# Gate, up and their gradients with rows on the partitions, turned by DMA in the first and the last phase of a layer's forward and backward pass

## The chip, the cores and the metric

The kernel runs on one NeuronCore of a Trainium2 chip. The metric is the device time of one execution in microseconds; for each kernel the median of several executions is given.

The engines have the names of the profile. PE is the matrix engine (PEld are its weight loads, the loads of the stationary operand), DVE is the vector engine, ACT the scalar engine, POOL the GpSimd engine, and SP the sync engine, which here only issues DMAs. An engine works through its own queue in order, and what waits at the head of a queue holds up everything behind it.

## The reference

`q`, `k`, `v`, `out` have S = 2048 rows and D = 1024 columns in bf16; the hidden width is F = 3584. The function is one layer, and the kernel gives its output and the gradients of all the inputs that take part:

```python
xn  = layernorm(q)
kv  = shift_conv(k, shift_k) * v              # a causal convolution with 4 taps per column
y   = irfft(rfft(kv) * rfft(ssm_k)) + kv * ssm_D    # a long convolution along the rows
g   = xn @ w_gate ; u = xn @ w_up             # [S, F]
h   = g * u
out = q + (xn * y) * silu(h @ w_down)
# and, for a given grad_out: dq, dk, dv, dshift_k, dssm_k, dssm_D, dw_gate, dw_up, dw_down
```

With `bm = h @ w_down` and its gradient `dbm`, the backward pass of the right-hand branch is `dh = dbm @ w_down.T`, `dg = dh * u`, `du = dh * g`, `dw_gate = xn.T @ dg`, `dw_up = xn.T @ du`, `dw_down = h.T @ dbm`, and `dxn` gets `dg @ w_gate.T + du @ w_up.T`. These matrix products are most of the work of PE. The long convolution is done as a transform in two steps, matmuls with tables and products on DVE.

## The kernel before

A matmul on PE sums over the partitions of its two operands. The stationary operand is at most 128 x 128; the moving one has up to 512 columns here; the result has the columns of the stationary operand on its partitions. So `h @ w_down` needs h with features on the partitions (`hT`), `h.T @ dbm` needs h with rows on the partitions; `xn.T @ dg` needs dg with rows on the partitions, `dg @ w_gate.T` needs it with features on the partitions. Each of h, dg and du is therefore needed in both layouts, and somebody has to turn it.

The 2048 rows are 16 blocks of 128 (`NB`), D is 8 chunks of 128 (`DC`), F is 28 chunks of 128 (`NF`) or 14 slabs of 256 (`NSL`, `SLW`). The time is spent in stages, one after the other on PE:

1. *Start*, 0 to 98.8 us. The layer norm runs over chunks of 2, 2, 4, 4 and 4 row blocks, on DVE and ACT; PE turns each normed block (`XNT`, columns of xn on the partitions, one tile for 4 row blocks), and the first two slabs of gate and up follow chunk by chunk. `load_bcast` spreads the convolution taps and `ssm_D` over the partitions by ten matmuls with a single row (line 149); it comes ahead of the first layer norm. `hrow`, `ssm_k` rows, is turned by PE transposes (line 628).
2. *Gate and up*, 98.8 to 570.4 us, slabs 2 to 13. `gu_unit` (lines 555 to 578) works on one chunk of 128 features and a half of the rows: a weight chunk stands in PE, 512 rows of `XNT` move, the result has features on the partitions. ACT copies it into `gut`, which goes to DRAM (`GUTd`, ACT's queue); DVE multiplies the two halves to `hT`, which goes to DRAM (`HTd`, POOL's queue). After each group of matmuls `tick` issues a share of the forward convolution (`make_pump`): DVE products, transform matmuls, and their DMAs, mostly on POOL's queue.
3. *Down matmul*, 570.4 to 773 us: `bm` from `HTd` (`bm_mm`, line 952) with w_down in the tiles `WD`, which lie in the buffers U6, U7, U2, U3, U9, U10 and U8; `gate` does silu and its derivative and stores `dbm`; PE turns dbm into `DBMT`.
4. *dh and dw*, 773 to 1474.6 us, slab by slab. `dh_half` (lines 1045 to 1071) loads g and u (`gul`), computes dh with features on the partitions (`wdt`, a transposed slab of w_down, is stationary, 512 rows of `DBMT` move), ACT copies it, DVE multiplies (line 1061, inside the helper on line 196). A deferred `turn` stores the products to `DGUTd` on ACT's queue, turns them by 16 PE transposes (line 1069) and two ACT copies (line 1070). `dw_slab` (lines 1073 to 1086) then computes dw_gate and dw_up of the slab from the turned tile. The half slab ahead is always computed before the `dw_slab` that uses the older ones. `btick` issues shares of the backward convolution between the groups; that is mostly work of DVE.
5. *dw_down*, 1474.6 to 1680.8 us: `h` with rows on the partitions comes from `HTd` by DMA transposes (`load_h`, line 1097). Towards its end, w_gate and w_up are loaded by DMA transposes (`WGU`, line 1136).
6. *dx*, 1680.8 us to the end: for each row block, 14 pieces of 4 x 2 matmuls (line 1203), with dg and du loaded from `DGUTd` (`load_dgut`), then `ln_backward` on DVE and ACT. The small matmuls of dk are put between.

`defer` and `flush` push a piece of work back by one or two groups of matmuls. `ld` issues on SP's queue, `st` and `cld` on POOL's, `sta` on ACT's; all DMA transposes go through SP's queue. Within an engine the order is what a scheduler makes of the program's order and of priorities (`high_priority`, `issue_after`). Most big operands live in buffers `U0` to `U10` of 8 KB a partition, each of which has one content after another; a load into one of them waits for the last reader of the content before.

## Time and profile before

| what | us |
|---|---|
| median of four executions | 2105.4 |
| the four executions | 2104.5, 2113.41, 2101.2, 2106.29 |
| the profiled execution | 2105.87 |
| its span | 2104.1 |

The mean clock granted to PE in the profiled execution was 0.993 of the full one. Times in the profile count from the start of the span. "Busy" of a group of instructions is the time in which its engine worked on it; matmuls overlap their neighbours, so a group's mean (379 ns for a matmul of 512 columns) is longer than the distance from one to the next. A line such as `L196` can be that of a helper that many places use; then the operands' names tell them apart. In the lines of groups, the last column is the time for which the engine had nothing to do just before an instruction of the group, with what ended it. Transfers are listed with their queue and with the median time from issue to landing.

### The profile page before, as it was taken

Reading aid. Unit: us, or ns where it says so; the run is one execution under the profiler, and the core shown is the slowest. Engines: PE = TensorE matmul, PEld = TensorE weight load, DVE = VectorE, ACT = ScalarE, POOL = GpSimd, SP = SyncE. Lnnn points to the kernel's source line nnn. Section 1 sums busy time; section 2 is a strip of 40 time slices with the busy share of each in tenths; the row PEclk is TensorE's granted clock in tenths of the full one; section 3 lists DMA queues with packets and bytes.
Section 4 is the critical chain, followed back from the end, with each engine's and each line's share of the span. In section 5 each row is a group of like instructions: output and inputs, shape, how many; then the busy total and the mean of one; then the engine's idle time right before and its main releaser. Section 6 shows DMA issues by size and latency. Waiting matters only on the chain.

```text
span 2104.1 us, 28251 instructions
## 1 busy us (share of the span) xinstructions
PE 2031.7 (97%) x11242; PEld 1033.7 (49%) x11242; DVE 1451.3 (69%) x1950; ACT 677.3 (32%) x1028; POOL 300.9 (14%) x448
## 2 busy tenths in 40 slices
PE   5999999999999999999999999999999999999998
PEld 4445555556444445555444444544444444444443
DVE  7779898978555556777999877987786025344432
ACT  4633433334333343444333343333122202111111
POOL 2211111110011120001021112111111101110100
PEclk9999999999999999999999999999999999999999
DMA  7666676456497877667788777756955995444431
GB/s 245 208 235 198 212 231 215 165 200 234 168 337 248 259 252 238 191 210 175 252 251 238 212 223 233 238 188 195 256 148 155 244 288 174 154 153 161 152 105 41
DMA packets 412789, 435.51 MB, mean 207 GB/s; under 512 B 178176, under 2 KB 326952, under 8 KB 401648
## 3 DMA queue, kind: packets, MB, share of 16 engines
q1 hardware_dynamic: 260816, 184.84, 31.0%
q0 software_dynamic: 40768, 174.40, 24.1%
q10 hardware_dynamic: 111072, 74.47, 11.7%
q8 instruction: 88, 1.44, 0.3%
q14 instruction: 45, 0.37, 0.0%
HBM read 221.78 MB, written 179.34 MB: 191 GB/s over the span
## 4 chain that ended last, share of the span: by engine, by line
PE 47%; DVE 24%; issue 19%; DMA 6%; POOL 2%; ACT 1%; SPq 1%; ACTq 0%; POOLq 0%; DVEq 0%
PE psx L1203 18%; PE psb L1170 9%; DVE m L196 7%; PE psg L565 7%; DVE W L196 5%; PE psb L1077 5%; DVE HX L196 3%; DMA B<-HFd 2%; PE psP L213 2%; PE psS L213 1%; PE psdk L927 1%; PE psb L1054 1%; DVE A L196 1%; DVE KX L196 1%; DVE B L196 1%
## 5 line engine op out<-in xcount | busy, mean ns | idle before, releaser
L565 PE MATMUL psg<-U,wslab 128*128 128x512 bf16 (+1 forms) x1856 | 406.7, 375 | 7.7 <-ACT guts L567 4.1
L1077 PE MATMUL psb<-U,U 128*128 128x512 bf16 x1792 | 399.6, 379 | 0.0
L1203 PE MATMUL psx<-U,dgut 128*128 128x512 bf16 x1408 | 308.5, 379 | 0.0
L565 PEld LDWEIGHTS <-wslab 128*128 128x128 bf16 x1856 | 182.8, 99 | 198.8 <-issue 9.2
L1203 PEld LDWEIGHTS <-dgut 128*128 128x128 bf16 x1792 | 175.3, 98 | 211.4
L1077 PEld LDWEIGHTS <-U 128*128 128x128 bf16 x1792 | 173.9, 98 | 194.2
L1054 PE MATMUL psb<-U,wdt 128*128 128x512 bf16 x896 | 208.1, 383 | 1.1 <-ACT bm L967 1.1
L1170 PE MATMUL psb<-U,U 128*128 128x512 bf16 x896 | 197.2, 379 | 2.8 <-DMA U<-HTd 2.8
L567 ACT CAST gut<-psg 128x512 bf16<-128x512 f32 x192 | 112.5, 587 | 223.5 <-PE psg L565 217.1
L952 PE MATMUL psbm<-U,ht 128*128 128x512 bf16 x784 | 171.8, 379 | 0.0
L1081 ACT CAST wb<-psb 128x512 bf16<-128x512 f32 x112 | 65.7, 587 | 267.3 <-PE psb L1077 225.0
L196 DVE TENSOR_TENSOR m<-A,B 128x1024 bf16<-128x1024 bf16 (+1 forms) x160 | 116.7, 793 | 44.1 <-issue 18.6
L196 DVE TENSOR_TENSOR W<-W 128x1024 f32<-128x1024 f32 (+1 forms) x144 | 139.5, 986 | 2.9
L1170 PEld LDWEIGHTS <-U 128*128 128x128 bf16 x896 | 86.7, 98 | 104.3 <-DMA U<-HTd 3.8
L1054 PEld LDWEIGHTS <-wdt 128*128 128x128 bf16 x896 | 87.5, 99 | 96.2 <-issue 5.5
L1226 ACT ACTIVATE dx_t<-dxn 128x1024 bf16<-128x1024 f32 (+1 forms) x17 | 17.1, 1007 | 345.4 <-DVE dxn L196 338.5
L952 PEld LDWEIGHTS <-ht 128*128 128x128 bf16 x784 | 76.1, 98 | 89.0
L196 DVE TENSOR_TENSOR dka<-dkh,Wbc 128x1024 bf16<-128x1024 bf16 x16 | 11.1, 692 | 156.9 <-DMA dkh<-DKSHd 156.9
L1070 ACT COPY U<-tr 128x1024 bf16<-128x1024 bf16 x112 | 109.4, 1022 | 17.7 <-PE tr L1069 6.1
L1056 ACT CAST dht<-psb 128x512 bf16<-128x512 f32 x112 | 65.3, 587 | 119.3 <-PE psb L1054 77.7
L196 DVE TENSOR_TENSOR gul<-gul,dht 128x2048 bf16<-128x2048 bf16 x56 | 69.6, 1243 | 29.9 <-ACT dht L1056 29.4
L1203 PE MATMUL psx<-W,dgut 128*128 128x512 bf16 x384 | 86.0, 379 | 0.0
(240 smaller groups left out, 2432.3 us busy)
## 6 DMA issues: line engine op xcount, KB each, us to landing
gul<-GUTd SPq DMA_DIRECT2D x56, 512.0 KB, 6.0
DGUTd<-gul ACTq DMA_DIRECT2D x56, 512.0 KB, 7.4
dgut<-DGUTd SPq DMA_DIRECT2D x16, 1792.0 KB, 8.6
GUTd<-gut ACTq DMA_DIRECT2D x48, 512.0 KB, 4.5
A<-DYFd POOLq DMA_DIRECT2D x16, 1024.0 KB, 5.7
out_dram<-wb ACTq DMA_DIRECT2D x224, 64.0 KB, 3.1
ht<-HTd SPq DMA_DIRECT2D x7, 1536.0 KB, 7.4
KFd<-KX POOLq DMA_DIRECT2D x8, 1024.0 KB, 4.5
```

The source lines that it names most:

```text
L196: V.tensor_tensor(o, a, b, op)
L213: nc.tensor.matmul(ps[:, k].rearrange("p (c d) -> p c d", c=2), T[:, r, k, :], xr[:, r], start=(n == 0), stop=(n == len(rs) - 1))
L565: nc.tensor.matmul(ps[:, 0:n], w[:, dc, a, fi * P:(fi + 1) * P], XNT[q][:, dc, qo:qo + n], start=(dc == 0), stop=(dc == DC - 1))
L567: nc.scalar.copy(out=gut[:, a, o:o + n], in_=ps[:, 0:n])
L952: nc.tensor.matmul(ps[:, dh * 512:(dh + 1) * 512], ht(fc)[:, i * P:(i + 1) * P], WD[fc // 4][:, fc % 4, dh * 512:(dh + 1) * 512], start=(f ...
L1054: nc.tensor.matmul(ps[:], wdt[:, dc, fi * P:(fi + 1) * P], DBMT[2 * hf + k][:, dc, :], start=(dc == 0), stop=(dc == DC - 1))
L1056: nc.scalar.copy(out=dht[:, k * 512:(k + 1) * 512], in_=ps[:])
L1070: nc.scalar.copy(out=dgu[:, :, a, fi * P:(fi + 1) * P], in_=ps[:])
L1077: nc.tensor.matmul(ps[:], XN[b // 4][:, b % 4, dc * P:(dc + 1) * P], dgus[b // 8][:, b % 8].rearrange("p a f -> p (a f)"), start=(b == 0), ...
L1081: nc.scalar.copy(out=wb[:].rearrange("p a f -> p (a f)"), in_=ps[:])
L1170: nc.tensor.matmul(ps[:], h(b, f), DBM[b // 4][:, b % 4, dh * 512:(dh + 1) * 512], start=(b == 0), stop=(b == NB - 1))
L1203: nc.tensor.matmul(ps[:, dh * 512:(dh + 1) * 512], t[a][:, 4 * j + f, i * P:(i + 1) * P], WGU[n][:, f, dh * 512:(dh + 1) * 512], start=(n ...
```

## The change

The rows take the place of the features on the partitions, wherever g, u, h and their gradients are computed.

- `gu_unit` keeps a block of 128 rows of `XNT` in PE and moves 512 columns, the up and the gate part of a slab. g and u go to `GUd`, and h, with rows on the partitions, to `Hd`. `turn_h` reads half a slab of `Hd` (1024 rows x 256 features, 0.5 MB) back by a DMA transpose on SP's queue and stores it to `HTd` on POOL's queue; `h_done` puts this off by one half slab.
- `dh_half` keeps a block of `DBMT` in PE and moves 256 columns of `wdt`: 1792 matmuls of 256 columns instead of 896 of 512. DVE multiplies in place in the tile that held g and u (`DGU`), and `dw_slab` reads that tile. The PE transposes and their copies are gone. The products are stored to `DGd`.
- `load_h` reads `Hd` without turning.
- `load_dgut` turns the gradients: 56 DMA transposes of 0.5 MB in the last phase, 14 for each group of 512 rows. dx works on pairs of row blocks.
- In the start, the products of `load_bcast` come behind the gate/up matmuls of the third and fourth chunk, and the turning of `hrow` behind the last layer-norm transposes.
- Buffers move: `v`, `acc` and `prod` of the convolution lie in U4 and U7, there are two more buffers (U11, U12), PSUM is shared out anew, and the pieces of `WGU` are loaded earlier in dw_down.

The core of the diff:

```diff
-    def gu_unit(fc, s0, ns, w, tick):
...
-                for dc in range(DC):
-                    nc.tensor.matmul(ps[:, 0:n], w[:, dc, a, fi * P:(fi + 1) * P], XNT[q][:, dc, qo:qo + n],
-                                     start=(dc == 0), stop=(dc == DC - 1))
-                nc.scalar.copy(out=gut[:, a, o:o + n], in_=ps[:, 0:n])
...
-        sta(GUTd[fc, :, :, s0:s0 + ns], gut[:, :, 0:ns])
...
+    def gu_unit(sl, b0, n, w, tick):
+
+        gut = fg.tile([P, 4, 2, SLW], BF16, name="gut")
+        hN = fg.tile([P, 4, SLW], BF16, name="hN")
+        for i in range(n):
+            q, qi = divmod(b0 + i, 4)
+            ps = ps_gu.tile([P, 512], F32, name="psg")
+            for dc in range(DC):
+                gu_mm[0] = nc.tensor.matmul(ps[:], XNT[q][:, dc, qi * P:(qi + 1) * P],
+                                            w[:, dc].rearrange("p a f -> p (a f)"), start=(dc == 0), stop=(dc == DC - 1))
+            nc.scalar.copy(out=gut[:, i].rearrange("p a f -> p (a f)"), in_=ps[:])
+            flush(2)
+            tick()
+        sta(GUd[sl, b0 // 8][:, b0 % 8:b0 % 8 + n], gut[:, 0:n])
+        tt(hN[:, 0:n], gut[:, 0:n, 0], gut[:, 0:n, 1], MUL)
+        st(Hd[sl, b0 * P:(b0 + n) * P, :].rearrange("(b u) f -> u b f", u=P), hN[:, 0:n])
+
+    hT_due = []
+
+    def turn_h(sl, hf):
+
+        hT = fg.tile([P, 2, 1024], BF16, name="hT")
+        nc.sync.dma_start_transpose(out=hT[:], in_=Hd[sl, hf * 1024:(hf + 1) * 1024, :])
+        fr = sl % 12 * SLW
+        st(HTd[hf][sl // 12][fr:fr + SLW, :].rearrange("(a f) s -> f a s", f=P), hT[:])
+
+    def h_done(sl, hf):
+
+        hT_due.append((sl, hf))
+        if len(hT_due) > 1:
+            turn_h(*hT_due.pop(0))
...
-    load_bcast(bsb, ps_st)
+    bcast = load_bcast(bsb, ps_st)
...
+        for sl in range(2):
+            gu_unit(sl, b0, n, slabs[sl], nop)
+            if i in (2, 3):
+                with tc.issue_after(gu_mm[0].ins):
+                    for j in ((3, 4), (2,), (1,), (0,))[2 * (i - 2) + sl]:
+                        bcast(j)
...
+    turn_h(*hT_due.pop())
     flush()
     drain()
...
-    def dh_half(fc, hf, wdt, dgu):
...
-            for a in range(2):
-                ps = ps_tr.tile([P, 8, P], BF16, name="tr")
-                for i in range(8):
-                    nc.tensor.transpose(ps[:, i, :], dgt[:, a, i * P:(i + 1) * P], ident[:])
-                nc.scalar.copy(out=dgu[:, :, a, fi * P:(fi + 1) * P], in_=ps[:])
-        defer(turn)
+    def dh_half(k, wdt):
+
+        sl, hf = divmod(k, 2)
+        dgu = DGU[k]
+        for g in range(2):
+            bs = slice(4 * g, 4 * g + 4)
+            dht = bg.tile([P, 4, SLW], BF16, name="dht")
+            for e in range(2):
+                ps = ps_b.tile([P, 512], F32, name="psb")
+                for x in range(2):
+                    b = 4 * g + 2 * e + x
+                    for dc in range(DC):
+                        nc.tensor.matmul(ps[:, x * SLW:(x + 1) * SLW], DBMT[2 * hf + g][:, dc, (b % 4) * P:(b % 4 + 1) * P],
+                                         wdt[:, dc, :], start=(dc == 0), stop=(dc == DC - 1))
+                nc.scalar.copy(out=dht[:, 2 * e:2 * e + 2].rearrange("p b f -> p (b f)"), in_=ps[:])
+                flush(2)
+                btick(1)
+            with tc.high_priority(60):
+                tt(dgu[:, bs], dgu[:, bs], dht[:].unsqueeze(2).to_broadcast([P, 4, 2, SLW]), MUL)
+
+        def store():
+            fs = slice(sl % 2 * SLW, sl % 2 * SLW + SLW)
             for a in range(2):
...
+                sta(DGd[sl // 2, a, 1024 * hf:1024 * hf + 1024, fs].rearrange("(b u) f -> u b f", u=P), dgu[:, :, a, :])
+        defer(store)
+        return dgu
...
+    def load_h(sl, home):
+        h = u8(home, "p (b f) -> p b f", b=NB)
+        ld(h, Hd[sl].rearrange("(b u) f -> u b f", u=P))
+        return h
...
+    def load_dgut(g, n):
+
+        a, j = pieces[n]
+        t = (gd, gd2)[n // 7].tile([P, 4, 512], BF16, name=f"dgut{n}")
+        nc.sync.dma_start_transpose(out=t[:], in_=DGd[j, a, 512 * g:512 * g + 512, :])
+        return t
...
+    ts = [load_dgut(0, n) for n in range(7)]
+    for i, j in enumerate((11, 0, 1, 4, 5)):
         load_wgu(9 + i, u8(j, a=4))
-    ts[1] = load_dgut(1)
...
+        ts.append(load_dgut(0, 7 + i))
+    ts += [load_dgut(0, n) for n in (12, 13)]
+    for g in range(4):
+        for b in (4 * g, 4 * g + 2):
+            if b == NB - 2:
+                break
+
+            pss = [ps_x.tile([P, D], F32, name="psx") for i in range(2)]
+            for n in range(14):
+                for i in range(2):
+                    dx_part(ts, b % 4 + i, pss[i], n)
+                if b % 4 == 2:
+                    ts[n] = load_dgut(g + 1, n)
+            for i in range(2):
+                with tc.high_priority(40):
+                    ln_backward(b + i, lambda h: pss[i][:])
```

## The prediction

> **What bounds the kernel now.** First the busy totals of the page:
>
> ```profile
> span 2104.1 us, 28251 instructions
> PE 2031.7 (97%) x11242; PEld 1033.7 (49%) x11242; DVE 1451.3 (69%) x1950; ACT 677.3 (32%) x1028; POOL 300.9 (14%) x448
> ```
>
> TensorE (PE) is busy for 97% of the span, so only less matmul work, or the 72 us in which it is idle, can make the kernel faster. Next the same by stage. A row holds the window, its length, then busy time and count of PE, PEld (weight loads), DVE, ACT and POOL, the granted clock, the DMA share and GB/s. The rows are the start, the gate/up phase, the dh/dw phase and the dx phase:
>
> ```profile
> 0.00:25.40 25.40, 8.60 (x45) 4.55 (x46) 19.82 (x68) 10.04 (x18) 8.71 (x20) 0.98 0.98 334
> 98.80:570.40 471.60, 457.76 (x2683) 258.99 (x2681) 406.25 (x518) 180.30 (x303) 71.36 (x114) 0.99 0.61 205
> 773.00:1474.60 701.60, 681.10 (x4073) 351.08 (x4073) 579.84 (x730) 276.32 (x415) 98.72 (x142) 0.99 0.73 223
> 1680.80:2104.10 423.30, 413.87 (x1918) 187.42 (x1916) 164.12 (x214) 57.61 (x86) 38.44 (x61) 0.99 0.48 154
> ```
>
> The average DVE share hides something. Cut into feature slabs, the dh/dw phase has DVE as full as PE in some of them:
>
> ```profile
> 806.20:857.50 51.30, 50.97 (x325) 27.24 (x323) 40.57 (x62) 21.19 (x34) 3.72 (x7) 1.00 0.68 209
> 1006.90:1057.90 51.00, 48.59 (x290) 24.48 (x289) 50.72 (x60) 19.09 (x29) 4.44 (x7) 1.00 0.79 241
> 1107.30:1159.00 51.70, 48.37 (x276) 24.83 (x274) 51.07 (x62) 18.89 (x30) 7.99 (x12) 0.97 0.80 237
> 1006.90:1356.70 349.80, 335.44 (x1937) 170.69 (x1936) 316.44 (x366) 133.76 (x202) 60.37 (x91) 0.99 0.76 230
> ```
>
> Slab 1 (first row) is PE's alone; in slabs 4 and 6 (next two) DVE is busy 50.72 of 51.00 and 51.07 of 51.70 us; the last row is slabs 4 to 10 together. Last, the groups that the change touches (busy time, mean ns; idle time before, and what ended it), and single stretches of PE's and SP's timelines:
>
> ```profile
> L1070 ACT COPY U<-tr 128x1024 bf16<-128x1024 bf16 x112 | 109.4, 1022 | 17.7 <-PE tr L1069 6.1 <-DVE W L196 5.2 <-PE psb L1077 2.8
> L196 DVE TENSOR_TENSOR gul<-gul,dht 128x2048 bf16<-128x2048 bf16 x56 | 69.6, 1243 | 29.9 <-ACT dht L1056 29.4
> L1069 PE MATMUL tr<-ident,gul 128*128 128x128 bf16 x896 | 60.9, 222 | 14.9 <-DVE gul L196 14.9
> L628 PE MATMUL tr<-ident,hrow 128*128 128x128 bf16 x128 | 10.9, 227 | 3.9 <-DMA hrow<-in_A_ssm_k_dram 3.8
> L149 PE MATMUL tr<-wrow,ones_row 1*128 1x512 bf16 x8 | 4.0, 614 | 13.0 <-DMA wrow<-in_A_shift_k_dram 9.0 <-ACT Wbc L150 4.0
> ```
>
> ```profile
> 33.81 7.15 PE L565 MATMUL psg<-U,wslab 128*128 128x256 bf16 x64
> 571.06 24.33 PE L952 MATMUL psbm<-U,U 128*128 128x512 bf16 x112 [0.67 <-ACT gut L567]
> 1064.76 1.06 PE L1069 MATMUL tr<-ident,gul 128*128 128x128 bf16 x16
> ```
>
> ```profile
> 580.56 10.08 SPq L62 DMA_DIRECT2D ht<-HTd  x2
> 1656.08 4.25 SPq L1136 DMA_TRANSPOSE W<-in_B_w_up_dram  x1
> 1660.55 4.20 SPq L1136 DMA_TRANSPOSE W<-in_B_w_gate_dram  x1
> ```
>
> Prices. A 512-column matmul: the chain of waits shows 96 of dx in 20.72 us, 215.8 ns each. A 256-column one with its own weight load: 7.15/64 = 112 ns, 4 ns over half of that. A PE transpose: the next stretch starts 0.89 us after 16 of them, 55.6 ns. A DMA transpose of 1 MB: about 4.2 us on SP's queue, so 2.1 for 0.5 MB.
>
> **The change part by part.** The profiled execution took 2105.9 us (span 2104.1), 0.5 above the median of the four runs; the sum goes against 2105.9.
>
> *Start (0 to 98.8).* The broadcast products (L149) cost PE 13.0 us of waiting ahead of the first gate/up work; they go behind chunks 2 and 3, and the hrow transposes (L628, 3.9 of waiting) behind the last layer-norm transposes. Both waits go, but the layer norm is late next: DVE is busy 19.8 of the first 25.4 us, and its chunks release PE one after the other. I take −7, a little under half of 16.9; ends −13 (the larger wait whole) and 0.
>
> *Gate/up (98.8 to 570.4).* Swapping the stationary operand leaves the count of 512-column matmuls, their copies and products as they are. New are 28 transposes of h on SP (28 × 2.1 = 59 us), 14.7 MB written to Hd, and POOL's wait for each transpose ahead of its store to HTd, with conv loads queued behind. PE's matmuls hide all of it: the DMA share is 0.61, and 59 more of 471.6 make 0.74. A slab's weights are asked for about two slabs ahead, so a transpose ahead of them on SP has a slab (about 34 us) of slack. With the cover gone, each of 28 could cost POOL about 4 us, but only conv loads feel it: ends 0 and +12; I take +3, near the covered end.
>
> *Turn to the down matmul (570.4).* Before, PE goes on after 0.67 us, with half of h long loaded and the last weight tiles (U8 to U10, via SP) just in time. Now the last half slab needs: ACT's copy 0.6, the product 0.7, the store's issue 0.55 and landing about 4.5 (256 KB stores of h: 4.3), the transpose 4 to 5.6, the store to HTd about 5: some 17 us. The last weight loads and the first ht tiles wait on SP behind that transpose, or for its buffer. The weights then land near 570.4 + 21.6; PE, with 13.8 us of matmuls on the earlier tiles, stalls about 7, and a little more for ht: +9. Ends: +6 (half the fill hidden again), and +16, since the last weight issue to ht's landing takes under 24 us in the before trace.
>
> *dh and dw (773 to 1474.6).* Gone are 896 PE transposes, 896 × 55.6 ns = 49.8 us of PE, and 112 ACT copies (109.4 us, off the path); 896 matmuls of 512 columns become 1792 of 256: 896 × 2 × 4 ns = +7 by 7.15/64, a stretch that also holds the fill of the first matmul; two halves at 215.8 give 0. I take +2. PE's 14.9 us of waits for the product lie mostly in slabs 4 to 10, where PE idles for 14.4 us; the weight-gradient matmuls now read the product itself, with a whole dh_half (7 us) between product and use, so elsewhere I add no wait.
> The DMA stores (1 MB per half slab) stay in size; gu loads become 28 of 1 MB instead of 56 of 0.5, issued two and a half slabs ahead.
> What DVE does is unchanged, and decides what of it is won. Slabs 4 to 10: 349.8 us, PE 335.4 − 7/14 × 49.8 + 1 = 312, DVE 316.4. Before, the span exceeded the larger of the two by 14.4 us; add 14 again to DVE's 316: 330, a gain of 20. Ends: 0 (DVE's order, not its total, sets the pace), 34 (no excess). Slabs 0 to 3, where PE alone is full: 4/14 × 47.8 = 14. Slabs 11 to 13: 10 by the same. Sum −44; ends −24 and −58.
>
> [...] The trace has 64 256-column matmuls with their own loads in 7.15 us. [...]
>
> *dw_down (1474.6 to 1680.8).* h comes by plain 1 MB loads instead of transposes, 512 bytes a run. PE is busy 203.35 of 206.2 already. 0; ends −2 and +5 (the first tiles late).
>
> *dx (1680.8 to the end).* The gradients now come by 56 DMA transposes of 0.5 MB: 56 × 2.1 = 118 us of SP in 413 us of PE. At the start 5 weight pieces and 7 gradient pieces need 5 × 4.3 + 7 × 2.1 = 36 us, where PE's first pair of rows offers 45: +1, ends 0 and +10. Later each piece has about 45 us until it is used. Rows go in pairs with 3 PSUM tiles; a pair's turn leaves 3.5 us (16 matmuls) for DVE's first read of 1.2 us: 0. If the pieces were late, PE waits, since nothing else is left but dk.
>
> [...]
>
> Sum: −7 + 3 + 9 − 44 + 0 + 1 = −38; 2105.9 − 38 = 2068.
>
> **The rivals.**
> A, the sum: 2068, own range 2052 to 2084.
>
> B, DVE holds slabs 4 to 10 at the old pace, so 20 of the 44 are lost: DVE's order of conv work and products is what slab 4's 50.72 of 51.00 speaks for; slabs 9 and 10, with DVE at 40 of 50, speak against. With the turn's upper end (+7): 2068 + 20 + 7 = 2095, range 2088 to 2100.
>
> C, all of PE's gain is won, and the start's: 2068 − 14 − 6 = 2048. For: DVE's 29.9 us of waiting before the product (for ACT), which has less to do now. Against: the excess of 14 was there before.
>
> D, slower: the dx phase is bound by its DMA transposes. Its first group of 14 pieces is consumed while the next arrives, and PE spends 4 × 14 × 8 × 0.2158 = 97 us on a group. Up to 97/14 = 6.9 us a piece PE is not held; the same 0.5 MB transposes of w_down took 8.1 us (median) from issue to landing. Should each wait for the one before to land, 56 × 8.1 = 454 us against 388 of dx matmuls: +66, 2134. It eats the whole gain of 38 from (388 + 38)/56 = 7.6 us. Against: consecutive transposes of 1 MB stand 4.2 us apart.
>
> E, no change: as B, and the start gains nothing either, because the layer norm alone sets it (+7): 2102.
>
> **How the numbers follow.** A 50%, B 18%, C 13%, D 11%, E 8%. About 0.5% (10.5 us) is what a measurement of this kernel can tell from no change. A, B and C are faster but for the upper edge of B: 0.79; E and that edge are the same: 0.09; D: 0.12. The range goes from C's lower middle, 2042, to E's upper edge, 2104; it leaves out D and the bottom of C, about 15%. The predicted time is A's.
>
> **What would show it.** PE's busy time near 1984 with no L1069 transposes; ACT near 568; slabs 0 to 3 about 3.5 us shorter each, slabs 4 to 10 about 3 with DVE at 95%; one PE wait of 6 to 16 us at the first down matmuls, ended by a weight load or ht; first gate/up matmuls before 20 us. The prediction is wrong if 256-column matmuls take over 120 ns, if slabs 4 to 10 keep 50 us, or if PE waits in dx for the transposed gradients.

## The result, and the profile after

The changed kernel takes 2116.05 us (median of 40 runs, 2103.03 to 2128.02), the kernel before 2102.86 us (median of 59). The ratio is 1.0058, with a 95% interval of 1.0046 to 1.0069: it is slower by half a per cent, where a gain of 38 us was forecast, and lies outside the range. The profiled execution took 2111.27 us with a span of 2109.1, 5.0 us over the one before.

The page's totals of the changed kernel:

```profile
span 2109.1 us, 28068 instructions
PE 1995.0 (95%) x11178; PEld 1065.8 (51%) x11178; DVE 1459.1 (69%) x1937; ACT 574.5 (27%) x911; POOL 329.5 (16%) x466
```

PE has 36.7 us less to do, and stands idle for 114.1 us instead of 72.4. The same by stage (columns as in the prediction: window, length, PE, PEld, DVE, ACT, POOL, clock, DMA share, GB/s). The windows are gate/up with the forward convolution, the down matmul, dh/dw, and dx:

```profile
88.00:592.00 504.00, 463.78 (x2682) 261.50 (x2683) 411.05 (x522) 180.69 (x304) 101.28 (x141) 0.96 0.82 243
592.00:815.40 223.40, 204.08 (x1027) 95.45 (x1026) 111.71 (x177) 65.29 (x65) 41.52 (x65) 0.97 0.86 272
815.40:1472.40 657.00, 634.63 (x4065) 389.18 (x4064) 581.14 (x721) 170.08 (x300) 97.13 (x139) 0.99 0.76 232
1675.90:2109.10 433.20, 416.36 (x1918) 187.37 (x1916) 164.18 (x214) 57.72 (x86) 38.41 (x61) 0.99 0.64 149
```

| stage | before | after | difference | forecast (ends) |
|---|---|---|---|---|
| start | 98.8 | 88.0 | −10.8 | −7 (−13 to 0) |
| gate/up with conv forward | 471.6 | 504.0 | +32.4 | +3 (0 to +12) |
| turn and down matmul | 202.6 | 223.4 | +20.8 | +9 (+6 to +16) |
| dh/dw | 701.6 | 657.0 | −44.6 | −44 (−58 to −24) |
| dw_down | 206.2 | 203.5 | −2.7 | 0 (−2 to +5) |
| dx | 423.3 | 433.2 | +9.9 | +1 (0 to +10) |

So the gain came where it was expected and in its full size. Most of it was given back in the stages into which the turning was moved, above all in gate/up. There the waits of three engines answer one another. In the changed kernel's list of waits (total, times, longest), PE, DVE and POOL in the gate/up window:

```profile
PE psP L216 <- DVE W L199: 23.4, 4, 9.7
PE psS L216 <- DVE kv L199: 7.9, 1, 7.9
...
DVE U L199 <- DMA k<-KSLd: 29.7, 3, 12.2
...
DVE kv L199 <- DMA U<-in_A_v_dram: 11.4, 1, 11.4
...
POOL HTd L65 <- DMA hT<-Hd: 211.2, 23, 15.4
```

PE stands in the convolution's transforms (line 216 of the changed kernel, 213 of the one before) because DVE is late, DVE is late because loads of k and v are, and POOL, on whose queue these loads are, waits 211 us for transposes of h. In the kernel before, the lists of PE and DVE for the same stage have these two lines, and POOL's has no wait for a turned tile:

```profile
PE psP L213 <- DVE W L196: 5.3, 3, 3.1
...
DVE prod L196 <- DMA k<-KSLd: 11.6, 4, 6.3
```

One such place in the changed kernel's POOL timeline, and what DVE then waited for:

```profile
239.80 0.71 POOL L65 DMA_DIRECT2D HTd<-hT  x1 [12.74 <-DMA hT<-Hd]
240.50 0.58 POOL L65 DMA_DIRECT2D k<-KSLd  x1
```

```profile
254.15 1.23 DVE L199 TENSOR_TENSOR U<-k,Wbc 128x2048 bf16<-128x2048 bf16 x1 [12.22 <-DMA k<-KSLd]
```

A load of k stands right behind the store that waits, and a second one at 244.2 us, in a row of issues that POOL lets go at once. DVE's wait ends when the second lands, 10.0 us after its issue. A PE wait of 9.7 us follows, which ends at 256.6.

The turn to the down matmul, on PE's and on SP's timeline, with the second wait that comes at the other end of this stage:

```profile
605.52 3.61 PE L974 MATMUL psbm<-U,U 128*128 128x512 bf16 x16 [1.92 <-DMA U<-in_B_w_down_dram]
618.27 12.61 PE L974 MATMUL psbm<-U,U 128*128 128x512 bf16 x48 [9.13 <-DMA U<-in_B_w_down_dram]
...
814.57 1.03 PE L1013 MATMUL psb<-ident,dbm 128*128 128x128 bf16 x8 [6.70 <-DVE dbm L199]
```

```profile
600.82 5.23 SPq L581 DMA_TRANSPOSE hT<-Hd  x1
...
612.55 1.49 SPq L62 DMA_DIRECT2D U<-in_B_w_down_dram  x3
```

The last transpose goes off at 600.8, and the last three loads of w_down at 612.6. In dx, PE waits 0.8, 5.1 and 1.6 us for the transposed gradients of its first pair of rows, and nowhere later:

```profile
1717.80 5.50 PE L1222 MATMUL psx<-U,dgut 128*128 128x512 bf16 x16 [5.13 <-DMA dgut<-DGd]
```

### The profile page after: what moved, and what is told of

The parts are those of the page before. It is cut to its first block, busy times and chain, and to the rows that moved or that the text cites. A ratio compares the mean times of both kernels' runs of the same rounds, so it can differ in the third digit from the quotient of the medians.

```text
span 2109.1 us, 28068 instructions
## 1 busy us (share of the span) xinstructions
PE 1995.0 (95%) x11178; PEld 1065.8 (51%) x11178; DVE 1459.1 (69%) x1937; ACT 574.5 (27%) x911; POOL 329.5 (16%) x466
## 4 chain that ended last, share of the span: by engine, by line
PE 41%; DVE 10%; issue 4%; DMA 2%; SPq 2%; POOL 1%; ACT 0%; ACTq 0%; DVEq 0%; POOLq 0%
PE psx L1222 17%; PE psb L1111 10%; PE psb L1191 9%; DVE W L199 4%; PE psb L1092 3%; DVE m L199 2%; SPq L1162 2%; DVE U L199 1%; PE psdk L949 1%; DMA dyl<-DYd 1%; DMA B<-HFd 1%; DVE B L242 1%; DVE A L199 1%; DVE B L199 1%; PE psY L914 1%
## 5 line engine op out<-in xcount | busy, mean ns | idle before, releaser
L567 PE MATMUL psg<-wslab,U 128*128 128x512 bf16 x1792 | 407.8, 382 | 3.3 <-ACT gut L569 1.6
L1222 PE MATMUL psx<-U,dgut 128*128 128x512 bf16 x1536 | 337.8, 381 | 7.5 <-DMA dgut<-DGd 7.5
L1111 PEld LDWEIGHTS <-U 128*128 128x128 bf16 x1792 | 176.1, 98 | 211.4 <-issue 16.7
L567 PEld LDWEIGHTS <-U 128*128 128x128 bf16 x1792 | 175.4, 98 | 199.3 <-issue 10.1
L1092 PE MATMUL psb<-wdt,U 128*128 128x256 bf16 x1792 | 206.0, 275 | 0.0
L569 ACT CAST gut<-psg 128x512 bf16<-128x512 f32 x224 | 130.7, 585 | 247.4 <-PE psg L567 243.3
L1092 PEld LDWEIGHTS <-U 128*128 128x128 bf16 x1792 | 176.2, 98 | 23.6
L1191 PEld LDWEIGHTS <-U 128*128 128x128 bf16 x896 | 86.9, 98 | 102.2
L199 DVE TENSOR_TENSOR dka<-dkh,Wbc 128x1024 bf16<-128x1024 bf16 x16 | 11.1, 692 | 174.5 <-DMA dkh<-DKSHd 174.5
L216 PEld LDWEIGHTS <-TF 128*128 128x128 bf16 x640 | 62.7, 102 | 60.7 <-DVE W L199 29.6
L199 DVE TENSOR_TENSOR U<-U,dht 128x2048 bf16<-128x2048 bf16 x56 | 68.2, 1221 | 23.5 <-ACT dht L1094 23.5
L199 DVE TENSOR_TENSOR gg<-bm,sig 128x1024 bf16<-128x1024 bf16 x16 | 11.0, 690 | 99.9 <-ACT sig L992 99.9
```

The lines of the kernel that those rows point to most:

```text
L199: V.tensor_tensor(o, a, b, op)
L216: nc.tensor.matmul(ps[:, k].rearrange("p (c d) -> p c d", c=2), T[:, r, k, :], xr[:, r], start=(n == 0), stop=(n == len(rs) - 1))
L567: gu_mm[0] = nc.tensor.matmul(ps[:], XNT[q][:, dc, qi * P:(qi + 1) * P], w[:, dc].rearrange("p a f -> p (a f)"), start=(dc == 0), stop=(dc ...
L569: nc.scalar.copy(out=gut[:, i].rearrange("p a f -> p (a f)"), in_=ps[:])
L1092: nc.tensor.matmul(ps[:, x * SLW:(x + 1) * SLW], DBMT[2 * hf + g][:, dc, (b % 4) * P:(b % 4 + 1) * P], wdt[:, dc, :], start=(dc == 0), sto ...
L1111: nc.tensor.matmul(ps[:], XN[b // 4][:, b % 4, dc * P:(dc + 1) * P], dgus[b // 8][:, b % 8].rearrange("p a f -> p (a f)"), start=(b == 0), ...
```

## The experiments

The theories at first: P, that POOL's queue is the cause in gate/up (convolution loads stand behind stores that wait for transposes); T, that the added traffic slows the loads in whatever order; M, that the swapped operands are slower on PE. Later C was added: transposes that are under way together with a burst of other transfers make both crawl. "Gate/up" below runs from the first matmul of slab 2 to the first down matmul, 472.3 us before and 505.1 after (good to some 2 us). Ratios are to the kernel before on the same chip.

**e1, the store of the turned h one half slab later on POOL's queue.**

`store_h` stores the half slab turned before, behind the newest store of h to Hd.

```diff
+            with tc.issue_after(hd_st[0].ins):
+                st(HTd[hf][sl // 12][fr:fr + SLW, :].rearrange("(a f) s -> f a s", f=P), hT)
...
     def turn_h(sl, hf):
 
+        store_h()
         hT = fg.tile([P, 2, 1024], BF16, name="hT")
         nc.sync.dma_start_transpose(out=hT[:], in_=Hd[sl, hf * 1024:(hf + 1) * 1024, :])
-        fr = sl % 12 * SLW
-        st(HTd[hf][sl // 12][fr:fr + SLW, :].rearrange("(a f) s -> f a s", f=P), hT[:])
+        hT_st.append((sl, hf, hT[:]))
```

> The store of the turned h to HTd is queued on POOL one half slab later, behind the next half slab's store of h, when its transpose should long have landed. All transfers and bytes stay. In the changed kernel POOL waits 211 us of the gate/up phase for transposes (88 to 592 us), and gate/up takes 504 us where it took 471.6 before. Theory P (POOL's queue: the convolution's loads of k and v and the stores of h stand behind the waiting store): POOL's wait for transposes falls below 50 us, DVE's waits for k and v (41 us) fall to about the 12 us of before, gate/up takes 470 to 482 us, and the whole is 22 to 34 us faster than the changed kernel, about 2085. Theory T (traffic: 28 transposes and 14.7 MB more keep the loads late, in whatever order): gate/up stays above 495 us, the whole within 10 us of the changed kernel. Theory M (the swapped operands are slower on PE): no change either, and PE busy per matmul stays up where nothing waits.

2102.76 us, ratio 0.9979 (0.9956 to 1.0003): 13 us less than the changed kernel. POOL's wait for transposes fell from 211 to 4.7 us, and from 140 us on no PE wait in gate/up exceeds 4.4 us. But gate/up is still 497.1, above the 495 that was set for T, because one wait of 22.5 us now stands at 110 to 132 us, where a load of k made DVE wait for 21.4. P is right for the later waits; the first one needs another cause.

**e2, no turning of h.** The transposes are left out; HTd gets g and u, straight from ACT's tile.

```diff
-        hT = fg.tile([P, 2, 1024], BF16, name="hT")
-        nc.sync.dma_start_transpose(out=hT[:], in_=Hd[sl, hf * 1024:(hf + 1) * 1024, :])
...
-        st(HTd[hf][sl // 12][fr:fr + SLW, :].rearrange("(a f) s -> f a s", f=P), hT[:])
+        flat = last_gut[0][:].rearrange("p b a s -> p (b a s)")
+        st(HTd[hf][sl // 12][fr:fr + SLW, :].rearrange("(a f) s -> f a s", f=P),
+           flat.rearrange("p (a s) -> p a s", a=2))
```

> Leaves out the 28 transposes of h: HTd gets the same 0.5 MB stores from POOL, but out of the tile of g and u that ACT has just written, so the values in HTd are not h. It shows what the transposes' own traffic costs. Theory P: gate/up takes 468 to 480 us, within 6 us of the late store. Theory T: gate/up falls by 20 us or more against the late store. Theory M: still about 504. At the turn to the down matmul PE's 11.7 us of waiting shrinks to some 3 to 6, since the last store to HTd no longer waits for a transpose.

2065.34 us (two executions), ratio 0.9806 (0.9776 to 0.9837), gate/up 468.9. M falls: the same matmuls with the same operands take no longer than before (472.3). Everything that was lost in gate/up hangs on the turning. The run does not tell P from T, since both the transposes' traffic and POOL's waits for them are gone. That the whole is within 3 us of the forecast is in part chance, as the forecast had 9 us for the turn to the down matmul, of which little is left here either (PE's waits for w_down are 2.7 us instead of 11.1).

**e3, the last half slab turned behind the loads of w_down; the last dbm block turned behind the first dh matmuls.**

```diff
-    turn_h(*hT_due.pop())
...
-    WD += [u8(j, a=4) for j in (2, 3, 9, 10, 8)]
+    WD += [u8(j, a=4) for j in (2, 3, 8, 9, 10)]
...
         ht1 = load_ht(1)
+    sl, hf = hT_due.pop()
+    hT = U[1][:, 0:2048].rearrange("p (a s) -> p a s", a=2)
+    with tc.issue_after(ht1[1].ins):
+        nc.sync.dma_start_transpose(out=hT, in_=Hd[sl, hf * 1024:(hf + 1) * 1024, :])
+    st(HTd[hf][sl // 12]..., hT)
...
-    flush()
     for k in (1, 2):
         gu_in(k)
```

> Only the stage change at 592 us and the one at 808 us are touched. The last half slab of h is turned into a free part of U1 behind the loads of w_down and of the first ht on SP, and the weight tiles are taken in the order U8, U9, U10; the turn of the last dbm block is no longer put ahead of the first dh matmuls. If the wait came from SP's order and from the buffer of the last transpose: PE's 11.7 us of waits for w_down fall to 0 to 3, and the 6.7 us for dbm to under 1.5; from the last gate/up matmul to the first dh matmul 204 to 209 us instead of 223.4; the whole 14 to 20 us faster than the changed kernel, about 2098. Rival (the wait is the late store of h and of y itself, behind POOL's waits, whatever stands on SP): 6 to 10 us of the first wait stay, and the whole gains 6 to 10.

2114.18 us, ratio 1.0033 (1.0011 to 1.0055). Place by place it did what it should: 11.7 us became 2.8, and 6.7 became 1.9 (the dbm turn) and 1.1. From the first down matmul to the first dh matmul it is 211.9 us instead of 222.3. A part came back at once, in e3's PE timeline, as the third row block waits for its dbm, whose inputs now stand behind ht and the last transpose on SP:

```profile
645.01 1.03 PE L1012 MATMUL tr<-ident,dbm 128*128 128x128 bf16 x8 [5.38 <-DVE dbm L199]
```

Some 5 us more came back in dh/dw (662.3 instead of 657.2), which now holds the turn of the last dbm block. So the price of the turn was read rightly, and of the 10 us saved there 2 show in the medians and some 4 in the profiled executions (2106.79 against 2111.27), which the spread does not tell from none.

**e4, dx starts with three row blocks.**

```diff
-        for b in (4 * g, 4 * g + 2):
+        for b, m in ((0, 3), (3, 1)) if g == 0 else ((4 * g, 2), (4 * g + 2, 2)):
...
-                if b % 4 == 2:
+                if b % 4 + m == 4:
                     ts[n] = load_dgut(g + 1, n)
```

> The dx phase only: the first pass takes three row blocks instead of two (5.2 us of PE per piece instead of 3.5), then one alone. If PE's 7.5 us of waits come from the start, where five weight pieces and seven gradient pieces follow one another on SP at some 6 us a pair: no wait is left, dx takes 423 to 427 us instead of 433.2, the whole is 6 to 10 us faster than the changed kernel. If the transposes are bound by their rate throughout: a wait of the same size comes back in the second pass, and the whole stays within 3 us.

2116.76 us, ratio 1.0044 (1.002 to 1.0068): nothing gained. The 7.5 us of waits for gradients are gone, and a wait of 9.9 us, at 1810 to 1820 us, for the dk units' load of dkh has taken their place; dx takes 435.1. The whole stayed where the second expectation had it, but not for its reason.

**e5, late store, and the turning of slabs 0 to 3 put off to slab 4 and later, two in each half slab.**

```diff
-        if len(hT_due) > 1:
+        if sl >= 4 and len(hT_due) > 1:
             turn_h(*hT_due.pop(0))
...
+            if sl >= 4 and len(hT_due) > 1:
+                turn_h(*hT_due.pop(0))
```

> The late store, and besides the first eight half slabs of h are not turned in slabs 0 to 3 but two by two from slab 4 on; transfers and bytes stay. With the late store alone PE still stood for 22.5 us at 110 to 132 us, while loads of k took up to 29 us to land, 256-byte transpose packets took 620 ns instead of 18, and the DMA moved 43 to 190 GB/s. Theory C (collision: three transposes in flight at once with the loads and stores at the start of the convolution make the DMA collapse): the 22.5 us and the slow clock behind it go, gate/up falls from 497 to 468 to 480 us, the whole is 25 to 35 us faster than the changed kernel, about 2085. Theory T (traffic): the transposes cost what they cost, wherever they lie: stalls of that size appear from slab 4 on, and gate/up stays at 488 or more.

The added turn stands between the two `gu_unit` calls of a half slab.

2108.17 us, ratio 1.0034 (1.0004 to 1.0063); gate/up 498.1. From 86 to 197 us, where no transpose of h runs, PE never waits longer than 0.9 us. Then, where two half slabs are turned in the time of one, the store follows its transpose too soon, POOL waits again (up to 15.9 us), and PE stands for 12.5 and 9.1 us. The total looks like T; the places speak for P and for C.

**e6, plain loads in place of the transposes of h** (the values in HTd are not turned).

```diff
-        nc.sync.dma_start_transpose(out=hT[:], in_=Hd[sl, hf * 1024:(hf + 1) * 1024, :])
+        ld(hT[:].rearrange("p a s -> p (a s)").rearrange("p (b f) -> p b f", b=8),
+           Hd[sl, hf * 1024:(hf + 1) * 1024, :].rearrange("(b u) f -> u b f", u=P))
```

> The changed kernel with each DMA transpose of h replaced by a plain load of the same 0.5 MB from the same place into the same tile, in runs of 512 bytes; the stores to HTd and all waits for them stay, so the values in HTd are not turned. Theory P (the wait in POOL's queue as such): POOL waits for the plain loads too, some 100 to 200 us, and gate/up stays at 490 or more. Theory T/C (the transposes, not the bytes): POOL's waits for it shrink to under 60 us, no collapse at 100 to 130 us, gate/up at 468 to 480.

2101.96 us, ratio 0.9995 (0.9971 to 1.002); gate/up 496.2. The list of POOL's waits in e6:

```profile
POOL HTd L65 <- DMA hT<-Hd: 205.8, 24, 14.4
```

POOL waits as long for plain loads as for transposes (211.2). Most of it is spent before the transfer starts, for it in turn waits for the store of h to Hd, which stands on POOL's own queue (SP waits 286.6 us for that in e6). SP's line in the changed kernel's list of waits:

```profile
SPq L581 <- DMA Hd<-hN: 260.5, 27, 27.7
```

Nor do the transfers themselves differ much by the median. From issue to landing the changed kernel's transposes of h have the first line below, and e6's plain loads the second (the last number is the median):

```profile
DMA to landing us min/median/max: 4.1/5.3/13.6
```

```profile
hT<-Hd SPq DMA_DIRECT2D x28, 512.0 KB, 5.1
```

PE stands for waits of 7.1 and 9.4 us that end at 247 and 372 us, as in the changed kernel, and the load of k behind the first of them takes 10.6 us to land with no transpose near it. This is P. At the start of the convolution the two waits are 3.3 and 6.1 us (7.9 and 4.6 with transposes). The kernel is 14 us faster than the changed one, so that turning by transposes does have a price beside that of the queue.

**e7, half of the product in dh** (half of the weight gradients are not gradients).

```diff
-                tt(dgu[:, bs], dgu[:, bs], dht[:].unsqueeze(2).to_broadcast([P, 4, 2, SLW]), MUL)
+                tt(dgu[:, bs, 0], dgu[:, bs, 0], dht[:], MUL)
```

> Leaves out half of the product in dh: only one of the two halves (u) of each tile is multiplied, so half of the weight gradients are not gradients. It takes about 28 us from DVE (56 x 0.5 us) in the dh/dw phase and nothing from PE. If DVE holds slabs 4 to 10 (330.0 us now, PE about 313 busy): those slabs lose 8 to 14 us, the first four slabs and the last three at most 1 to 3 together. If PE and its waits for the weight gradients' operands hold them: slabs 4 to 10 stay within 4 us of 330.

Slabs 4 to 10 in the changed kernel, and then in e7:

```profile
1030.90:1360.90 330.00, 312.64 (x1922) 189.07 (x1920) 316.62 (x368) 81.05 (x144) 60.17 (x93) 0.98 0.81 244
```

```profile
1053.60:1371.50 317.90, 309.50 (x1921) 188.77 (x1921) 296.81 (x360) 80.55 (x146) 59.56 (x91) 0.98 0.82 243
```

Taking 20 us from DVE shortens them by 12.1 while PE has the same matmuls: DVE does hold them. The kernel as a whole was slower, 2140.76 us (two executions; 1.0191, 1.017 to 1.0213), in part for a reason that belongs to the edit. The half that is no longer multiplied can be stored early, and ACT got stuck in issuing such a store, just ahead of the slabs measured above. It is seen on e7's ACT and PE timelines:

```profile
1041.62 11.21 ACTq L68 DMA_DIRECT2D DGd<-U  x1
```

```profile
1053.57 6.80 PE L1111 MATMUL psb<-U,U 128*128 128x512 bf16 x22 [10.61 <-ACT dht L1094]
```

**e8, e5 with e3, and h of dw_down in three buffers instead of four so that one weight piece of dx is loaded at slab 9.**

```diff
-    HSL = (3, 11, 6, 2)
+    HSL = (3, 11, 6)
...
+        if k == 9:
+            load_wgu(6, u8(2, a=4))
```

> The late and spread turning of h, the last half slab turned behind the loads of w_down into U1, the last dbm block turned behind the first dh matmuls, and h of dw_down in three buffers instead of four, so that one more weight piece of dx is loaded at slab 9. By theory C: gate/up 468 to 480, the down stage 206 to 212, dx 427 to 432 us; the whole about 2070 to 2080, faster than both kernels. By theory T: about 2100.

2105.26 us, ratio 0.9994 (0.9964 to 1.0025), gate/up 510.5 with PE waits of 13.4, 8.9 and 10.5 us from 244 us on: no better, as e5.

**e9, the store of the turned h on SP's queue.** One word of the changed kernel.

```diff
-        st(HTd[hf][sl // 12][fr:fr + SLW, :].rearrange("(a f) s -> f a s", f=P), hT[:])
+        ld(HTd[hf][sl // 12][fr:fr + SLW, :].rearrange("(a f) s -> f a s", f=P), hT[:])
```

> The changed kernel with one edit: the store of the turned h to HTd goes out on SP's queue, directly behind its transpose, instead of POOL's. So POOL waits for no transpose, SP does, where only the weights of a slab ahead stand behind; and a transpose is sent off only when the one before has been turned and its store is issued, so that never two or three are under way at once. Transfers and bytes stay. Theory P with C (POOL's queue, and the collision of several transposes with the backlog that it lets go at once): no PE wait over 5 us in the gate/up phase, which takes 470 to 482 us instead of 505, the whole 20 to 33 us faster than the changed kernel, 2083 to 2096. Theory T (the traffic itself, as e6 with plain loads at 496 us could also be read): gate/up stays at 490 or more. If SP takes POOL's place as the one that holds things up: PE waits for wslab.

2086.02 us, ratio 0.9922 (0.9899 to 0.9946): 30 us less than the changed kernel, and faster than the kernel before. (The profiled execution, 2094.88, is among its slowest; the stages are read from it.) The transfers and bytes are the same, and from 131 us on no PE wait in gate/up exceeds 1.9 us, which speaks against T. One wait is left, of 22.9 us at 107 to 130 us, so gate/up takes 490.9 us: not the 482 or less that was expected, and still within the 490 or more set for T. T falls only with e14 and e15, which move the same bytes in 477.8 and 469.1 us. In e9's list of waits, and among its DMA issues at 93 to 110 us (queue, count, size, median us to landing):

```profile
PE psP L216 <- DVE W L199: 24.4, 3, 22.9
```

```profile
k<-KSLd POOLq DMA_DIRECT2D x2, 352.0 KB, 22.5
...
hT<-Hd SPq DMA_TRANSPOSE x1, 30.6
```

The transpose before had landed by then (its store goes off at 94.4 us, this one at 94.9), so here one transpose beside the burst was enough. It is issued at the same time as the loads of k, which POOL no longer holds back: at 95.9 us, where in the changed kernel they left at 112.1.

**e10, e9 with e3 and the earlier weight piece.**

> The store on SP, the last half slab of h turned behind the loads of w_down into U1, the last dbm block turned behind the first dh matmuls, h of dw_down in three buffers so that one more weight piece of dx is loaded at slab 9. By P with C: gate/up 470 to 482, the down stage 206 to 212 instead of 222, dx 430 to 435; the whole 2070 to 2085, faster than both kernels. By T: about 2100, no better than the kernel before.

2083.31 us, ratio 0.9902 (0.9871 to 0.9933): gate/up 490.5 with a first wait of 19.0 us, down 211.4.

**e11, no turning in dx** (dx is not dx).

```diff
-        nc.sync.dma_start_transpose(out=t[:], in_=DGd[j, a, 512 * g:512 * g + 512, :])
+        ld(t[:], DGd[j, a, 512 * g:512 * g + 512, :].rearrange("(b u) f -> u b f", u=P))
```

> Leaves out the turning of the gradients in dx: the 56 DMA transposes become plain loads of the same 0.5 MB into the same tiles, so dx is not dx. dx takes 433 us in the changed kernel and 423 in the one before. If the transposes on SP make the difference: PE's 7.5 us of waits for the gradients go, dx 423 to 427, the whole 6 to 10 us faster than the changed kernel. If the weight pieces alone hold up the start: waits of 4 to 7 us stay, now for the weight pieces, dx 429 or more.

dx takes 423.0 us and PE waits for no gradient: the 10 us of this stage are the transposes' at its start. The whole is 2108.95 us (1.0044, 1.002 to 1.0067), 7 less than the changed kernel, though the intervals of the two ratios overlap.

**e12, e9 with the transposes moved out of slab 2.** Those of four half slabs were to come one by one in slabs 3 to 7.

> The store on SP as before, and the transposes of (slab 0, second half) and the three half slabs behind it are not sent off in slab 2, where the convolution starts, but one extra each in slabs 3 to 7. Everything else, transfers and bytes among it, stays. With the store on SP alone PE still stood 22.9 us at 107 to 130 us, behind a load of k that was issued at 97 us and landed at 121, while two transposes were under way. Theory C (a transpose under way together with the burst of loads and stores at the convolution's start makes both crawl): no PE wait over 5 us before 200 us, gate/up 491 -> 465 to 474 us, the whole 12 to 25 us faster than the store on SP alone, about 2064 to 2074. If the burst alone is the cause (the products of the start come some 10 us earlier than in the kernel before and meet the loads): a wait of 10 us or more stays at 100 to 135 us and the whole stays within 8 us of 2086.

2087.62 us, ratio 0.9923 (0.99 to 0.9947). The edit missed its aim: the scheduler put two of them on SP at 90 us all the same, where they took 28 us. PE stood for 10.3 us, waiting for ACT, which waited 11.7 us for a store of g and u to land, and gate/up takes 484.9.

**e13, the same with e3 and the earlier weight piece.**

> The same with the last half slab of h turned behind the loads of w_down, the last dbm block turned behind the first dh matmuls, and the earlier weight piece of dx. By C: gate/up 465 to 474, the down stage 206 to 212, the whole 2055 to 2070. If the burst alone is the cause: about 2080.

2083.57 us, ratio 0.9894 (0.9869 to 0.9919); gate/up 476.1, down 209.4. The first wait is 7.0 us, from the same two transposes.

**e14, as e12, with an edge on SP's queue that keeps the transposes behind the weights of slab 4.** Slab 3 sends off none either, and slabs 4 to 8 catch up.

```diff
-        if len(hT_due) > 1:
-            turn_h(*hT_due.pop(0))
+        if len(hT_due) > 1 and (sl, hf) != (1, 1) and sl not in (2, 3):
...
+                with tc.issue_after(slab_in[0].ins):
+                    turn_h(*hT_due.pop(0))
```

`slab_in[0]` is SP's newest load of a weight slab.

> In e12 the edit did not reach its aim: two transposes stood in SP's order at 90 us all the same, took 28 us there, the DMA moved 91 to 160 GB/s at 95 to 110 us, and PE stood for 10.3 us. Here the transposes are tied behind SP's load of the weights of slab 4, which comes when slab 2 is done; nothing else differs. Theory C (transposes under way in the convolution's first burst of loads and stores): DMA at 300 GB/s or more from 95 to 110 us, as in e5, where no transpose ran there; no PE wait over 3 us before 130 us; gate/up 465 to 474 us (491 with the store on SP alone), the whole 2060 to 2074. If the burst alone is the cause: a PE wait of 8 us or more stays at 100 to 135 us.

Now the transposes are out of that stretch. The stretch from 95 to 110 us in e12 and in e14:

```profile
95.00:110.00 15.00, 7.83 (x45) 4.40 (x45) 4.60 (x4) 1.75 (x3) 4.79 (x7) 0.91 1.22 130
```

```profile
95.00:110.00 15.00, 13.10 (x81) 7.29 (x80) 11.75 (x13) 6.34 (x10) 5.82 (x9) 1.00 0.98 341
```

and the loads of k in e14 at 93 to 110 us:

```profile
k<-KSLd POOLq DMA_DIRECT2D x2, 352.0 KB, 5.8
```

With two transposes under way the DMA engines count as busier (1.22) and move 130 GB/s; without them 341. POOL issues the same loads and stores at nearly the same times up to 103 us in both. The loads of k land in 5.8 us instead of 17.9 in e12 and 22.5 in e9, PE waits 1.9 us there, and gate/up takes 477.8. At this place it is C, and the burst alone is not the cause. A wait of 5.7 us is left that ends at 234 us, with transposes caught up in pairs. The profiled execution is 13 us shorter than that of e9 (2081.61 and 2094.88), but the one is among the faster of its kernel and the other among the slower, and the medians do not separate e9, e12 and e14: 2086.02, 2087.62 and 2089.63 (0.9936, 0.9912 to 0.996). What C costs the whole kernel is not shown.

**e15, e14 with e3 and the earlier weight piece.**

> The same with the last half slab of h turned behind the loads of w_down, the last dbm block turned behind the first dh matmuls, and the earlier weight piece of dx. By C: gate/up 465 to 474, the down stage 206 to 212, the whole 2052 to 2068, some 2% faster than the kernel before. Otherwise about 2080.

2080.65 us, ratio 0.9897 (0.9877 to 0.9918): faster than both kernels, by 1.0% and about 1.6%, but not by the 2% expected. Gate/up is 469.1, less than in the kernel before, and down 211.1; dh/dw takes 672.4, 15 more than in the changed kernel, with PE waits of 5.0 and 2.3 us in its first slabs. Why, was not followed up. e10, e13 and e15 cannot be told from one another by their medians.

## Why the prediction was wrong

**The step that failed is gate/up, and in it this sentence:** "With the cover gone, each of 28 could cost POOL about 4 us, but only conv loads feel it: ends 0 and +12; I take +3, near the covered end." Three things were wrong in it.

- The size. POOL waited 211 us in 23 waits, 9.2 each. The 4 us were the landing of a transpose; POOL waited from the time it reached the store, through the landing of h in Hd, which its own queue had delayed. e6 has the same wait without any transpose of h.
- The cover. "PE's matmuls hide all of it" took PE's own work for the cover. But the loads feed DVE, which was busy for 406 of 471.6 us before, and DVE feeds transform matmuls that stand in PE's queue in order. A load of k that came later than DVE's slack allowed stopped PE: behind DVE's wait of 12.2 us there is one of 9.7 on PE. e9, which changes the queue of 28 stores, gets back 14 us of gate/up in its profiled execution and 30 of the whole by the medians.
- Meeting. I priced a transpose as time on SP's queue, 2.1 us by the distance of two in a quiet stretch. In the changed kernel 0.5 MB took 5.3 us to land by the median and 13.6 at the convolution's start. In e9, where it met the loads of k, it took 30.6, and PE stood for 22.9 us there (1.9 in e14). In the changed kernel itself this is the smaller part, since its first two waits are 7.9 and 4.6 us, and 3.3 and 6.1 with plain loads (e6). The DMA share of 0.74 that I worked out said nothing of that.

With the queue and the meeting mended, gate/up is at 477.8 and 469.1 us (e14, e15) against 472.3 before, so +3 would have been about right for another order of the queues. One slip changes nothing: a slab of this stage lasts 39 us (12 of them in 471.6), not about 34, so the slack of the weight loads was larger than I took it to be.

**The turn to the down matmul** was right in mechanism and size: +9 forecast, 11.7 instead of 0.7 measured, on the chain that was named, and e3 takes it away. The stage as a whole lost 20.8 us, more than the end of +16. Not in the sum was its second end. The changed kernel takes PSUM for the last dbm block from the same pool as dh, and puts its turn ahead of the first dh matmuls, so PE waits 6.7 us for dbm, where it had waited 1.1. The diff showed the shared pool, and I read it as a matter of space.

**dh and dw** were right: −44 forecast, −44.6 measured. A 256-column matmul costs half of a 512-column one here, 115 ns of busy time against 232, as the group in the changed kernel and the one that it replaces show:

```profile
L1092 PE MATMUL psb<-wdt,U 128*128 128x256 bf16 x1792 | 206.0, 275 | 0.0
```

```profile
L1054 PE MATMUL psb<-U,wdt 128*128 128x512 bf16 x896 | 208.1, 383 | 1.1 <-ACT bm L967 1.1
```

Slabs 4 to 10 take 330.0 us, as forecast from DVE's work plus the old excess of 14, and e7 shows that DVE is what holds them. Slabs 0 to 3 gained 11.1 (14 forecast) and slabs 11 to 13 gained 6.4 (10); the 7.3 us ahead of slab 0, which nobody had named, made up for both. So the mechanism held, and that the total fits to within a microsecond is luck. The 1792 weight loads in place of 896 do not show in PE's time either: it is 206.0 us against 208.1.

**The start** gained 10.8, within its ends.

**dw_down** gained 2.7, a little more than the end of −2: PE is busy for 203.4 of 203.5 us there. **dx** lost 9.9, at the upper end of 0 to +10, and at the place that the forecast had looked at: at the start weight and gradient pieces follow one another on SP, and PE's first pair of rows, with the 45 us allowed for it, did not cover them. e11 shows that it is the transposes, since with plain loads dx takes 423.0 us. PE waiting in dx for the transposed gradients was one of the signs named for a wrong prediction. It came, with 7.5 us, but it is not what the forecast failed by. Rival D, the rate of the transposes throughout, did not happen: after the first pair no wait is left.

**The clock** was missing from the sum. PE is busy for 1995.0 us where 1984 were forecast, at a granted clock of 0.980 instead of 0.993. The 11 us come on top of the added waits, and they lie where the waits are: PE's busy time is up by 6.0 us in gate/up, 3.7 in the down stage and 2.5 in dx, with nearly the same matmuls. So these waits were paid twice: in the 4 us right behind the waits of 7.9, 9.7, 9.1, 6.7 and 5.1 us, the granted clock was 0.50 to 0.52. From the changed kernel's PE timeline, behind another one:

```profile
125.37 1.04 PE L216 MATMUL psP<-kv,TF 128*128 128x256 bf16 x4 [4.61 <-DVE W L199]
126.20 3.62 PE L567 MATMUL psg<-wslab,U 128*128 128x512 bf16 x8
...
131.17 1.89 PE L567 MATMUL psg<-wslab,U 128*128 128x512 bf16 x8
```

Eight matmuls take 3.62 us right behind a wait of 4.61 us, at a granted clock of 0.50, and 1.89 us five us later, at 1.00.

Of the rivals, the one on the slower side was put in dx, at a place with 97 us of cover for each group. Gate/up, with a queue shared by two chains, was the place for it.

## What to carry to other kernels

When a change puts a store that waits for a transfer on a queue, ask first whose loads stand behind it, and how much slack the consumer of those loads has. That the engine at the end of the chain is busy nearly all the time (PE for 97% of the span here) is no cover. Moving such a store to a queue on which only far-ahead loads wait can be worth more than the change itself (one word, 30 us here). Price a DMA transpose by its landing time among the transfers that will run beside it (5.3 us by the median here, 30.6 in e9's burst), not by the distance of two transposes on an idle queue (priced at 2.1), and look for the places where it meets a burst of loads that somebody waits for.

## What the runs showed of the hardware

- DMA transposes in the midst of a burst pulled down all the traffic: 130 GB/s with two under way and 341 without, in the same 15 us at the start of the convolution (e12 and e14), and 363 in e5, which has none there either. Not everywhere: the changed kernel moves 310 GB/s from 520 to 550 us with two transposes of h, which land in 6.5 us. What makes the difference is open. By the median the 28 transposes of h land in nearly the same time (5.3 us) as e6's plain loads of the same bytes (5.1); the one in e9's burst took 30.6.
- Issuing a DMA held an engine for long in one place: ACT stood 11.2 us in a single issue of a 0.5 MB store (e7), where the same instruction takes 0.4 us by the median of the 56 in the changed kernel.
- Repeated executions of these kernels mostly spread by 15 to 30 us, so that gains of 5 to 10 us, seen clearly at their place in a trace, do not show in medians of five to ten runs (e3, e4, e14).
